# Attention and two MLP blocks on one core: batch 0 takes its first channel group alone, batch 1 follows later, batch 3's heads are spread out

## The chip, the core and the metric

The kernel runs on one core of one Trainium2 chip. Five engines matter. TensorE (PE in the profile, its weight loads PEld) multiplies, VectorE (DVE), ScalarE (ACT) and GpSimd (POOL) work element by element, and SyncE's queue (SP) issues nearly all DMAs. Each engine takes its instructions in one fixed order. The metric is the time of one execution in device microseconds; lower is better.

## The reference, cut to what matters

```
attn = softmax_with_cap(q, k, cap) @ v      # 4 batches, 12 heads, 448 tokens, 64 per head
x    = heads side by side                   # (4, 448, 768)
xn   = (x - mean) / sqrt(var + 1e-6) * g    # over the 768 channels
x    = x + relu(xn @ w_ch1) @ w_ch2         # 768 -> 3072 -> 768
xt   = x transposed                         # tokens last
u    = x + transposed(relu(xt @ w_tok1) @ w_tok2)   # 448 -> 256 -> 448
out  = u + relu(u @ w2_ch1) @ w2_ch2        # 768 -> 1536 -> 768
```

All inputs and outputs are fp32. One batch is one attention, one normalisation, one channel MLP, one token mixing and one second channel MLP, in this order.

## The kernel before

A batch's x lies transposed in SBUF, channels on the partitions in six blocks of 128, tokens along the row (448). Products are made with fp32r operands in three passes: each operand is split into a high part and a low remainder, and high by high, low by high and high by low are added up. Batches 0 and 1 make their attention in plain fp32 (`early`), batches 2 and 3 in split passes.

**Channel MLP.** `mlp(plan, ends)` goes through groups of four hidden blocks. There are six groups in the first MLP (`NG1`) and three in the second (`NG2`). A group is four tiles of `w1` (18 passes of 448 columns for each batch, L541) and six tiles of `w2` (12 passes for each batch, L562), so 144 passes for each batch. What comes out of a `w1` tile is rectified by ACT (L546), and its remainder made by DVE (L547); what comes out of a `w2` tile is added to x by DVE (L566). A plan entry names a group and the batches that take it: a pair such as (0, 1) uses each loaded weight tile twice, a single batch once.

**Weights.** `load` brings a weight tile the first time through `piece`. It loads the raw words (L263), lets ACT work twice (L264, L265) and DVE three times (L266 to L268), then makes the high copy (L164 on ACT or L166 on DVE) and the low remainder on DVE (L160). A `w1` tile is two such pieces of 384 columns, a `w2` tile one of 512, so a group has 14 pieces. The result is kept in DRAM (L288), and every later use of the tile only loads it again (L284). Three split buffers hold tiles at one time.

**Attention.** A head is scores (L351 in fp32, L354 in split passes), tanh and exp on ACT (L357, L358), maxima on DVE (L362, L365), values (L372, or L393 to L396), and two DVE reads of the result (L400, L403). After six heads `divide` spreads the reciprocal sums with three fp32 products (L429) and scales x (L432).

**Normalisation.** `layer_norm` adds the six blocks (L457), subtracts the mean (L447), squares, adds (L469), and takes the root; `normalise` scales (L504) and splits into `big` (L506 and L160). `LN_ENGINES` puts the adds, subtractions and remainders of batch 0 on POOL and those of the others on DVE or POOL as the planner finds.

**Order.** Nothing runs in the order of the code. Each step has a key (`prog.key`, less an `early` lead), and `Program.emit` is a list scheduler with its own costs (`FIXED`, `RATE`). It takes the step whose engine is free first, and among the ready ones that with the least key. The order that comes out is fixed in the program. The keys are set at the end of the kernel, where each stage has a start and a pace.

Before, attention 0 and 1 with their normalisations come first. The pair (0, 1) then goes through all six groups of the first MLP beside the heads of batches 2 and 3, both batches mix tokens together, and the pair takes the second MLP's three groups. After that come the normalisations of batches 2 and 3 and the same for that pair, with batch 2 one group ahead.

Of the kernel before, what the change touches and what calls it, by code (L numbers as in the profile page):

```python
# [9 lines left out]
F32 = mybir.dt.float32  # L10
# [49 lines left out]
URGENT, SCORES, PREPARE, LOAD = 1000.0, 19.31, 4.58, 24.58  # L60
LEAD, RAW_AHEAD, EVACUATE, TOKENS_AHEAD = 6.3, 9.57, -7.49, 17.25
# [10 lines left out]
class Step:  # L72
    def __init__(self, engines, run, key):
        self.engines, self.run, self.key = engines, run, key
        self.waits, self.users, self.ready = 0, [], 0.0
        self.flexible = run.__code__.co_argcount > len(run.__defaults__ or ())


class Program:
# [4 lines left out]
    FIXED = {"pe": 0.0, "act": 0.19, "dve": 0.08, "pool": 0.16, "dma": 0.3}  # L84
    RATE = {"pe": 203e-3 / S, "act": 0.83e-3, "dve": 1.2e-3, "pool": 2.5e-3, "dma": 2.9e-3}
# [5 lines left out]
    def add(self, engine, cols, run, reads=(), writes=(), early=0.0, release=0.0):  # L91
# [3 lines left out]
        names = [name.split("*") for name in engine.split("/")]  # L95
        costs = {e: self.FIXED[e] + self.RATE[e] * cols * (0.5 if half else 1.0) for e, *half in names}
        step = Step(costs, run, (self.key - early, len(self.steps)))
        step.ready = release
# [14 lines left out]
    def emit(self):  # L113
        free = {e: 0.0 for e in self.FIXED}
# [9 lines left out]
        for _ in self.steps:  # L124
# [5 lines left out]
            free[e] = end = t + step.engines[e]  # L130
# [9 lines left out]
def block_kernel(ctx: ExitStack, tc: tile.TileContext, qkv, cap, gln, w1, w2, wt1, wt2, con, out):  # L140
# [116 lines left out]
    def piece(src, m, target, to):  # L257
# [8 lines left out]
        add("dve", m // 2, lambda: dve.tensor_scalar(f, f, 3, None, op0=ALU.logical_shift_left), (), [w])  # L266
        add("dve", m, lambda: dve.scalar_tensor_tensor(f, hi, -(1 << 31), f, op0=ALU.bitwise_and, op1=ALU.bitwise_or), [r], [w])  # L267
        add("dve", m, lambda: dve.tensor_tensor(f, f, lo, op=ALU.add), [r], [w])  # L268
        g = f.bitcast(F32)
        add("act/dve*", m, lambda e: copy(e, target[:, 0], g), [w], to)  # L270
        add("dve", m, lambda e: low(engine_of[e], target[:, 1], g, target[:, 0]), [w], to)
# [45 lines left out]
    def attention(b, start, pace):  # L317
# [7 lines left out]
        def head(h):  # L325
# [3 lines left out]
            add("dma", 960, lambda: nc.sync.dma_start(out=qk.at, in_=qkv[b, h, :, :S + 4 * P]), (), [qk], early=LOAD)  # L329
            add("dma", 384, lambda: nc.sync.dma_start(out=v.at, in_=qkv[b, h, :, S + 4 * P:].rearrange("p (c d) -> p c d", c=4)), (), [v], early=LOAD)  # L330
            q, k = qk.at[:, :S], qk.at[:, S:]
            if not early:
# [3 lines left out]
                add("dve/pool", 4 * P, lambda e: low(engine_of[e], ks.at[D:], k[D:], ks.at[D:]), [qk], [ks], early=PREPARE)  # L336
# [405 lines left out]
```

## Time and profile before

| what | value |
|---|---|
| median of 3 runs | 1439.97 us (1437.99 to 1440.24) |
| the profiled execution | 1440.12 us, of which its span 1438.1 us |
| busy in the span | PE 1397.5, PEld 1186.4, DVE 891.0, ACT 591.7, POOL 153.7 us |
| granted TensorE clock, mean | 0.986 |
| moved by DMA | 230.71 MB, mean 160 GB/s |

The span runs from the first to the last instruction; what lies around it is 2.0 us. Matmuls are pipelined and their records overlap, so the busy time of PE says little by itself: the number of passes in a stretch says more.

### The profile page before, as it was taken

Reading aid. Unit: us, or ns where it says so; the run is one execution under the profiler, and the core shown is the slowest. Engines: PE = TensorE matmul, PEld = TensorE weight load, DVE = VectorE, ACT = ScalarE, POOL = GpSimd, SP = SyncE. Lnnn points to the kernel's source line nnn. Section 1 sums busy time; section 2 is a strip of 40 time slices with the busy share of each in tenths; the row PEclk is TensorE's granted clock in tenths of the full one; section 3 lists DMA queues with packets and bytes.
Section 4 is the critical chain, followed back from the end, with each engine's and each line's share of the span. In section 5 each row is a group of like instructions: output and inputs, shape, how many; then the busy total and the mean of one; then the engine's idle time right before and its main releaser. Section 6 shows DMA issues by size and latency. Waiting matters only on the chain.

```text
span 1438.1 us, 17738 instructions
## 1 busy us (share of the span) xinstructions
PE 1397.5 (97%) x6560; PEld 1186.4 (83%) x6560; DVE 891.0 (62%) x1521; ACT 591.7 (41%) x947; POOL 153.7 (11%) x117
## 2 busy tenths in 40 slices
PE   8998799999999999999999989999999999999998
PEld 3343488888898888878889978999999999999997
DVE  5898799899999898898886883122121222432221
ACT  7885376757664666576543521100101001211000
POOL 0042121112114011011000141000000000000000
PEclk9998899999999999999999999999999999999999
DMA  5564146666574757651475736332332425354366
GB/s 180 166 204 131 38 138 205 214 214 210 184 230 152 249 167 229 193 160 37 141 242 171 238 142 203 103 128 89 116 125 84 130 96 159 126 175 137 118 197 197
DMA packets 116631, 230.71 MB, mean 160 GB/s; under 512 B 9024, under 2 KB 61504, under 8 KB 116544
## 3 DMA queue, kind: packets, MB, share of 16 engines
q1 hardware_dynamic: 115968, 229.28, 49.7%
q8 instruction: 52, 0.85, 0.2%
q10 hardware_dynamic: 576, 0.29, 0.1%
q14 instruction: 35, 0.29, 0.1%
HBM read 167.41 MB, written 62.13 MB: 160 GB/s over the span
## 4 chain that ended last, share of the span: by engine, by line
PE 88%; DVE 8%; DMA 1%; issue 1%; ACT 1%; ACTq 0%; DVEq 0%
PE bank L541 36%; PE bank L562 34%; PE bank L372 4%; PE sc L354 3%; PE bank L636 2%; PE bank L617 2%; PE bank L396 2%; PE bank L395 2%; DVE m L362 1%; PE sc L351 1%; PE bank L429 1%; PE bank L393 1%; DVE whole L267 1%; DVE split L160 1%; DVE area L504 1%
## 5 line engine op out<-in xcount | busy, mean ns | idle before, releaser
L562 PE MATMUL bank<-h,split 128*128 128x448 f32 x2592 | 550.6, 370 | 3.6 <-ACT split L164 1.6
L541 PE MATMUL bank<-big,split 128*128 128x448 f32 x2592 | 548.0, 370 | 4.6 <-DMA split<-kept 1.8
L541 PEld LDWEIGHTS bank<-big,split 128*128 128x128 f32 x2592 | 489.7, 189 | 50.9 <-POOL big L160 2.6
L562 PEld LDWEIGHTS bank<-h,split 128*128 128x128 f32 x2592 | 488.1, 189 | 51.4 <-issue 8.7
L546 ACT ACTIVATE h<-bank 128x448 fp32r<-128x448 f32 x144 | 78.4, 545 | 437.7 <-PE bank L541 437.4
L566 DVE TENSOR_TENSOR x<-x,bank 128x448 f32<-128x448 f32 x216 | 133.4, 618 | 189.8 <-PE bank L562 187.3
L547 DVE SCALAR_TENSOR_TENSOR h<-bank,h 128x448 fp32r<-128x448 f32 x144 | 89.4, 621 | 214.1 <-ACT h L546 213.8
L264 ACT ACTIVATE whole<-raw 128x384 f32<-128x384 f32 (+2 forms) x130 | 77.9, 600 | 54.3 <-DVE split L160 51.0
L164 ACT ACTIVATE split<-whole 128x384 fp32r<-128x384 f32 (+1 forms) x92 | 52.2, 567 | 92.7 <-PE bank L562 63.3
L160 DVE TENSOR_TENSOR split<-whole,split 128x384 fp32r<-128x384 f32 (+1 forms) x126 | 86.5, 690 | 3.9 <-ACT split L164 3.1
L268 DVE CUSTOM_DVE_ANT_0 whole<-raw,whole 128x768 uint16<-128x768 uint16 (+2 forms) x130 | 85.4, 658 | 3.1
L267 DVE SCALAR_TENSOR_TENSOR whole<-raw,whole 128x384 int32<-128x384 int32 (+2 forms) x130 | 85.0, 656 | 0.9
L265 ACT ACTIVATE raw<-raw 128x384 int32<-128x384 uint32 (+2 forms) x130 | 77.5, 598 | 0.0
L160 POOL TENSOR_TENSOR ks<-area,ks 64x512 fp32r<-64x512 f32 x23 | 32.8, 1427 | 351.9 <-ACT ks L335 351.9
L362 DVE TRANSPOSE_TENSOR_REDUCE m<-x 128x28 f32<-128x896 f32 x48 | 52.9, 1104 | 13.9 <-ACT x L358 13.6
L266 DVE TENSOR_SCALAR whole<-whole 128x384 int32<-128x384 int32 (+2 forms) x130 | 57.7, 445 | 4.7 <-ACT whole L264 4.2
L357 ACT ACTIVATE area<-sc,tsc 128x896 f32<-128x896 f32 x48 | 48.4, 1008 | 26.6 <-DVE el L160 13.6
L357 ACT ACTIVATE x<-sc,tsc 128x896 f32<-128x896 f32 x48 | 48.0, 1000 | 21.5 <-PE sc L351 11.0
L362 DVE TRANSPOSE_TENSOR_REDUCE m<-area 128x28 f32<-128x896 f32 x48 | 53.0, 1104 | 5.7 <-ACT area L358 5.7
L358 ACT ACTIVATE x<-x,cap_t 128x896 f32<-128x896 f32 x48 | 49.7, 1040 | 1.0
L358 ACT ACTIVATE area<-area,cap_t 128x896 f32<-128x896 f32 x48 | 49.9, 1040 | 0.4
L380 ACT ACTIVATE eh<-area 128x896 fp32r<-128x896 f32 x48 | 45.4, 946 | 5.8 <-PE bank L395 5.6
(109 smaller groups left out, 1177.3 us busy)
## 6 DMA issues: line engine op xcount, KB each, us to landing
split<-kept SPq DMA_DIRECT2D x96, 384.0 KB, 3.9
split<-kept SPq DMA_DIRECT2D x72, 512.0 KB, 3.7
raw<-in_w SPq DMA_DIRECT2D x72, 384.0 KB, 3.4
kept<-split SPq DMA_DIRECT2D x72, 384.0 KB, 3.2
raw<-in_w SPq DMA_DIRECT2D x54, 512.0 KB, 4.1
kept<-split SPq DMA_DIRECT2D x54, 512.0 KB, 3.3
area<-in_qkv SPq DMA_DIRECT2D x38, 480.0 KB, 3.7
area<-in_qkv SPq DMA_DIRECT2D x35, 192.0 KB, 3.4
```

The costliest lines, as they stand in the source:

```text
L160: eng.tensor_tensor(out, whole, high.bitcast(F32), op=ALU.subtract)
L264: add("act", m, lambda: act(f.bitcast(F32), hi.bitcast(F32), AF.Copy, scale=2.0 ** -112), [r], [w])
L267: add("dve", m, lambda: dve.scalar_tensor_tensor(f, hi, -(1 << 31), f, op0=ALU.bitwise_and, op1=ALU.bitwise_or), [r], [w])
L268: add("dve", m, lambda: dve.tensor_tensor(f, f, lo, op=ALU.add), [r], [w])
L357: add("act", 2 * S, lambda e=e, sc=sc: act(e, sc.at[:, :, :S], AF.Tanh, scale=tsc), [sc], eb)
L358: add("act", 2 * S, lambda e=e: act(e, e, AF.Exp, scale=cap_t), (), eb)
L362: add("dve", 2 * S, lambda half=half, e=e: dve.tensor_reduce(m.at[:, half].rearrange("p c j -> p (c j)"), e.rearrange("p c (j i) -> p (c j ...
L541: mm(ph.at[:, :S], w[:, wi, cc * P:(cc + 1) * P], src[cc].at[:, xi], start=(cc, n) == (0, 0), stop=(cc, n) == (NCC - 1, 2))
L546: add("act", S, lambda ht=ht, ph=ph: act(ht.at[:, 0], ph.at[:, :S], AF.Relu), [ph], [ht], early=EVACUATE)
L547: add("dve", S, lambda ht=ht, ph=ph: dve.scalar_tensor_tensor(ht.at[:, 1], ph.at[:, :S], 0.0, ht.at[:, 0].bitcast(F32), op0=ALU.max, op1=A ...
L562: mm(py.at[:, :S], w[:, wi, i * P:(i + 1) * P], h[i].at[:, hi], start=(i, n) == (0, 0), stop=(i, n) == (G - 1, 2))
L566: add("dve", S, lambda x=x, py=py: dve.tensor_tensor(x.at, x.at, py.at[:, :S], op=ALU.add), [py], [x], early=EVACUATE)
```

## The change

- `prepare(g)` converts the ten tiles of group 0 in advance, from key 14 on, beside attention 0, and keeps them in DRAM.
- Group 0 of the first MLP is taken by batch 0 alone (`groups((0,), 0, n0)`), from key 85, beside attention 1. The pair takes groups 1 to 5.
- Batch 1 takes group 0 while batch 0 mixes tokens. Batch 0 takes the first two groups of the second MLP while batch 1 mixes tokens; the pair takes the third; batch 1 then takes the first two alone.
- Batch 2 now takes two groups ahead (`N1` = 2 in place of 1), the first of them written ahead of batch 3's normalisation.
- The heads of batch 2 get the pace 25 in place of 20.29, those of batch 3 the start 560 and the pace 30 in place of 629.68 and 20.29.
- All of `LN_ENGINES` is DVE.
- In `divide`, the reciprocal sums are split into a high part (ACT) and a low one (DVE), and each of the three products is two fp32r passes in place of one fp32 product.
- The planner's costs change, and steps marked "+" take turns on a port that it now plans for.

```diff
+N0, N1, N2 = 1, 2, 2
+T_LN0, T_LN1 = 7.69, -20.0
+T_AHEAD, N_AHEAD, AHEAD_PACE = 14.0, 1, 5.0
+T_ALONE, STRETCH0, T_PAIR, STRETCH1 = 85.0, 1.3, 165.0, 1.14
+T_ATT2, PACE2, T_ATT3, PACE3 = 171.18, 25.0, 560.0, 30.0
...
+            d = el.at[:NH6]
+            add("act", S, lambda: act(d[:, 0], whole, AF.Copy), [sq], [el])
+            add("dve+", S, lambda: low(dve, d[:, 1], whole, d[:, 0]), [sq], [el])
...
-                    mm(pc.at[:, :S], pair_r[:NH6, pr].bitcast(F32), whole, start=True, stop=True)
+                    for i in range(2):
+                        mm(pc.at[:, :S], pair_r[:NH6, pr], d[:, i], start=i == 0, stop=i == 1)
...
-    LN_ENGINES = ["pool", "dve/pool", "dve/pool", "dve/pool"]
+    LN_ENGINES = ["dve+"] * 4
...
+    def prepare(g):
+        nonlocal n_tile
+        rows = [(w1, g * G + i, C) for i in range(G)] + [(w2, g * NCC + e, G * P) for e in range(NCC)]
+        for w, row, cols in rows:
+            load(n_tile, w, row, cols)
+            n_tile += 1
+            prog.key += AHEAD_PACE
...
-        attention(2, 171.18, 20.29)
+        n0, n1, n2 = N0, N1, N2
+        prog.key, stretch = T_ALONE, STRETCH0
+        weave(mlp(groups((0,), 0, n0)))
+        attention(2, T_ATT2, PACE2)
         layer_norm(2)
-        attention(3, 629.68, 20.29)
-        prog.key, stretch = 152.9, 1.14
-        weave(mlp(groups((0, 1), 0, NG1)))
-        weave(tokens(0, HIDDEN[1]), tokens(1, HIDDEN[2]))
-        weave(mlp(groups((0, 1), NG1, NG2), (0, 1)))
-        prog.key += 59.58
+        attention(3, T_ATT3, PACE3)
+        prog.key, stretch = T_PAIR, STRETCH1
+        weave(mlp(groups((0, 1), n0, NG1 - n0)))
+        weave(tokens(0, HIDDEN[2]), mlp(groups((1,), 0, n0)), ahead=TOKENS_AHEAD)
+        weave(tokens(1, HIDDEN[2]), mlp(groups((0,), NG1, n2)), ahead=TOKENS_AHEAD)
+        weave(mlp(groups((0, 1), NG1 + n2, NG2 - n2), (0,)))
+        weave(mlp(groups((1,), NG1, n2), (1,)))
         normalise(2)
+        stretch = 1.0
+        weave(mlp(groups((2,), 0, n1)))
         layer_norm(3)
         normalise(3)
-        prog.key, stretch = 966.61, 1.0
-        n1, n2 = 1, 2
-        weave(mlp(groups((2,), 0, n1) + groups((2, 3), n1, NG1 - n1)))
+        weave(mlp(groups((2, 3), n1, NG1 - n1)))
```

Three places show how the order moves. The first is TensorE in attention 1, around the sum of the squares of batch 0's normalisation; `sc` and `bank` are PSUM, `big` is the normalised x of batch 0, `split` a weight tile. Before, it stands so:

```order
L474 MATMUL bank_113<-inv_c,area 112x2 x4
L372 MATMUL bank_111<-x_82,x_83 96x448 x2
L372 MATMUL bank_111<-x_83 96x448 x2
L351 MATMUL sc_114<-x_83 128x448 x2
L494 MATMUL bank_112<-area,ones 128x448
L351 MATMUL sc_115<-x_83 128x448 x2
L411 MATMUL bank_110<-kc,rs_103 84x32
L412 MATMUL bank_110<-kc,rm_105 84x128
L351 MATMUL sc_114<-area 128x448 x2
L351 MATMUL sc_115<-area 128x448 x2
L541 MATMUL bank_112<-big_84,split_77 128x448 x6
L429 MATMUL bank_111<-area,pair_r 128x448
```

And now, from the same square sums (L487) on:

```order
L507 MATMUL bank_112<-area,ones 128x448
L360 MATMUL sc_115<-x_83 128x448 x2
L381 MATMUL bank_110<-x_82,x_83 96x448 x4
L360 MATMUL sc_114<-area 128x448 x2
L563 MATMUL bank_112<-big_84,split_78 128x448 x12
L563 MATMUL bank_113<-big_84,split_79 128x448 x12
L360 MATMUL sc_115<-area 128x448 x2
L381 MATMUL bank_111<-x_82,x_83 96x448 x2
L381 MATMUL bank_111<-x_83 96x448 x2
L360 MATMUL sc_114<-x_83 128x448 x2
L360 MATMUL sc_115<-x_83 128x448 x2
L563 MATMUL bank_112<-big_84,split_78 128x448 x6
```

Passes of the MLP (L541 before, L563 now) moved ahead of the sixth head's sums, between the scores and the values of attention 1.

The second place is VectorE at the third and fourth head of attention 0; `m`, `rm` and `rs` are maxima and sums of a head, `whole` and `raw` a weight piece under conversion. Before:

```order
L365 TENSOR_REDUCE rm_104<-m_101 128x14
L362 TENSOR_REDUCE m_100<-x_82 128x28 x2
L400 TENSOR_REDUCE rs_102<-bank_111 32x14
L403 COPY x_80<-bank_111 64x448
L365 TENSOR_REDUCE rm_104<-m_100 128x14
L362 TENSOR_REDUCE m_101<-x_82 128x28
```

And now:

```order
L275 TENSOR_SCALAR whole_75<-whole_75 128x384
L371 TENSOR_REDUCE m_100<-x_82 128x28
L276 SCALAR_TENSOR_TENSOR whole_75<-raw_72,whole_75 128x384
L409 TENSOR_REDUCE rs_102<-bank_111 32x14
L412 COPY x_80<-bank_111 64x448
L277 ISA whole_75<-raw_72,whole_75 128x768
L275 TENSOR_SCALAR whole_76<-whole_76 128x384
L175 CAST split_77<-whole_75 128x384
L276 SCALAR_TENSOR_TENSOR whole_76<-raw_73,whole_76 128x384
L169 TENSOR_TENSOR split_77<-whole_75,split_77 128x384
L277 ISA whole_76<-raw_73,whole_76 128x768
L371 TENSOR_REDUCE m_100<-x_82 128x28
```

Steps of the conversion (L275 to L277, L175, L169) moved in between the maxima of the heads.

The third place is TensorE where batch 1 mixes tokens, now beside batch 0's passes of the second MLP; L636 (now L658) is the mixing's second product, `t` and `h` its weights and hidden rows, L442 are the passes of `divide` for batch 3.

Before, the same second product stands so, the two batches by turns:

```order
L636 MATMUL bank_112<-t_71,h_86 128x448 x3
L636 MATMUL bank_112<-t_71,h_87 128x448 x3
L354 MATMUL sc_115<-qs_95,ks_96 128x448 x4
L636 MATMUL bank_113<-t_71,h_90 128x448 x3
L636 MATMUL bank_113<-t_71,h_91 128x448 x3
L636 MATMUL bank_111<-t_71,h_86 128x448 x3
L636 MATMUL bank_111<-t_71,h_87 128x448 x3
L636 MATMUL bank_112<-t_71,h_90 128x448 x3
```

And now, for batch 1 alone:

```order
L563 MATMUL bank_112<-big_84,split_77 128x448 x12
L563 MATMUL bank_111<-big_84,split_78 128x448 x6
L658 MATMUL bank_112<-t_71,h_92 128x448 x3
L658 MATMUL bank_112<-t_71,h_93 128x448 x3
L563 MATMUL bank_111<-big_84,split_78 128x448 x12
L442 MATMUL bank_110<-el_99,pair_r 128x448 x2
L563 MATMUL bank_113<-big_84,split_79 128x448 x6
L658 MATMUL bank_111<-t_71,h_92 128x448 x3
L658 MATMUL bank_111<-t_71,h_93 128x448 x3
```

No MLP pass stood among the mixing of batches 0 and 1 before. Now passes of batch 0's second MLP moved in between, and batch 0's own mixing is ahead of this place, among batch 1's passes of group 0.

## Rows read from the trace of the kernel before

**Rows 1.** The page's first part: busy us, share of the span, instructions.

```profile
PE 1397.5 (97%) x6560; PEld 1186.4 (83%) x6560; DVE 891.0 (62%) x1521; ACT 591.7 (41%) x947; POOL 153.7 (11%) x117
```

**Rows 2.** Stages: us, busy PE, PEld, DVE, ACT, POOL; clock, DMA share, GB/s.

```profile
8.00:66.00 58.00, 56.96 (x185) 23.05 (x183) 44.17 (x68) 47.34 (x52) 2.60 (x2) 1.00 0.53 174
66.00:126.00 60.00, 53.60 (x174) 23.47 (x173) 57.09 (x96) 46.00 (x63) 25.86 (x21) 0.91 0.53 164
126.00:186.00 60.00, 47.92 (x160) 27.00 (x159) 47.58 (x78) 27.87 (x38) 11.59 (x8) 0.87 0.23 71
...
303.20:381.30 78.10, 78.10 (x374) 68.02 (x373) 72.55 (x121) 53.01 (x85) 16.53 (x10) 1.00 0.60 193
...
618.60:723.70 105.10, 101.74 (x515) 88.59 (x515) 91.99 (x160) 67.86 (x113) 11.95 (x8) 1.00 0.33 105
...
798.80:868.90 70.10, 65.59 (x314) 59.00 (x314) 58.80 (x94) 27.01 (x51) 25.05 (x19) 0.98 0.52 177
868.90:899.30 30.40, 28.57 (x134) 25.99 (x133) 7.27 (x11) 2.26 (x5) 0.72 (x1) 0.94 0.68 222
```

**Rows 3.** The chain that ended last: start us, us, what.

```profile
11.45 2.97 PE bank L372 x7
...
14.79 1.50 PE sc L351 x7
...
51.34 0.95 PE bank L429 x2
...
769.00 29.18 PE bank L562 x144
```

**Rows 4.** The page's fifth part: DVE's four steps of a weight piece.

```profile
L160 DVE TENSOR_TENSOR split<-whole,split 128x384 fp32r<-128x384 f32 (+1 forms) x126 | 86.5, 690 | 3.9 <-ACT split L164 3.1
L268 DVE CUSTOM_DVE_ANT_0 whole<-raw,whole 128x768 uint16<-128x768 uint16 (+2 forms) x130 | 85.4, 658 | 3.1
L267 DVE SCALAR_TENSOR_TENSOR whole<-raw,whole 128x384 int32<-128x384 int32 (+2 forms) x130 | 85.0, 656 | 0.9
...
L266 DVE TENSOR_SCALAR whole<-whole 128x384 int32<-128x384 int32 (+2 forms) x130 | 57.7, 445 | 4.7 <-ACT whole L264 4.2
```

**Rows 5.** Groups by form: busy us, mean ns of one, idle before.

```profile
L362 DVE TRANSPOSE_TENSOR_REDUCE m<-x 128x28 f32<-128x896 f32 x48 | 52.9, 1104 | 13.9 <-ACT x L358 13.6
...
L160 POOL TENSOR_TENSOR qs<-area,qs 128x448 fp32r<-128x448 f32 x23 | 34.4, 1494 | 31.5 <-DVE qs L166 18.5 <-issue 8.1 <-ACT qs L164 3.4
L160 POOL TENSOR_TENSOR ks<-area,ks 64x512 fp32r<-64x512 f32 x23 | 32.8, 1427 | 351.9 <-ACT ks L335 351.9
...
L400 DVE TRANSPOSE_TENSOR_REDUCE rs<-bank 32x14 f32<-32x448 f32 x48 | 31.1, 648 | 21.0 <-PE bank L396 16.0 <-PE bank L372 2.9 <-PE sc L351 1.0
L403 DVE COPY x<-bank 64x448 f32<-64x448 f32 x48 | 29.6, 617 | 0.9
...
L457 DVE TENSOR_TENSOR area<-area,x 128x448 f32<-128x448 f32 x5 | 3.1, 621 | 0.1
```

**Rows 6.** Timeline: start us, us, then the operation.

```profile
88.51 5.18 POOL L447 TENSOR_TENSOR area<-x,mean 128x448 f32<-128x448 f32 x4 [3.81 <-ACT mean L459]
...
88.82 1.25 DVE L160 TENSOR_TENSOR split<-whole,split 128x384 fp32r<-128x384 f32 x1
...
123.83 0.55 DVE L160 TENSOR_TENSOR split<-whole,split 128x384 fp32r<-128x384 f32 x1
...
226.97 0.62 DVE L566 TENSOR_TENSOR x<-x,bank 128x448 f32<-128x448 f32 x1
...
617.99 0.62 DVE L566 TENSOR_TENSOR x<-x,bank 128x448 f32<-128x448 f32 x1 [0.64 <-PE bank L562]
...
868.29 0.61 DVE L566 TENSOR_TENSOR x<-x,bank 128x448 f32<-128x448 f32 x1
```

**Rows 7.** Line 566: least, median and longest ns, first and last start us.

```profile
L566 DVE TENSOR_TENSOR x<-x,bank x216: 581/620/622, 212.3 to 1434.4; 128x448 f32<-128x448 f32 x108
```

**Rows 8.** The busiest 10 us of DMA up to 500 us (columns of rows 2).

```profile
380.00:390.00 10.00, 10.00 (x51) 9.06 (x50) 9.01 (x19) 7.02 (x11) 0.00 (x0) 1.00 0.93 291
```

More of the change, by code (lines that the diff above doesn't have):

```diff
@@ L89, in __init__, with add @@
         self.steps, self.key = [], 0.0
-    def add(self, engine, cols, run, reads=(), writes=(), early=0.0, release=0.0):
-        names = [name.split("*") for name in engine.split("/")]
-        costs = {e: self.FIXED[e] + self.RATE[e] * cols * (0.5 if half else 1.0) for e, *half in names}
+    def add(self, engine, cols, run, reads=(), writes=(), early=0.0):
+        names = [(name.strip("*+"), "*" in name, "+" in name) for name in engine.split("/")]
+        costs = {e: self.FIXED[e] + self.RATE[e] * cols * (0.5 if half else 1.0) for e, half, _ in names}
         step = Step(costs, run, (self.key - early, len(self.steps)))
-        step.ready = release
+        step.port = {e for e, _, port in names if port}
         before = set()
@@ L113, in emit @@
     def emit(self):
-        free = {e: 0.0 for e in self.FIXED}
+        free, port = {e: 0.0 for e in self.FIXED}, 0.0
         queue = {e: [] for e in self.FIXED}
@@ L129, in emit @@
             step.run(e) if step.flexible else step.run()
-            free[e] = end = t + step.engines[e]
+            if e in step.port:
+                t = port = max(t, port) + step.engines[e]
+            else:
+                t += step.engines[e]
+            free[e] = end = t
             end += self.LATER.get(e, 0.0)
@@ L407, in divide @@
             hs = slice(6 * grp, 6 * grp + 6)
-            p, (r,), (sq,) = next(side_banks), R, SQ
+            p, (r,), (sq,), (el,) = next(side_banks), R, SQ, EL
             def gathered():
@@ L567, in mlp @@
                     if b in ends and b in final:
-                        add("dma", S, lambda b=b, e=e, x=x: nc.sync.dma_start(out=out[e, :, b], in_=x.at), [x], ())
+                        add("dma", S // 2, lambda b=b, e=e, x=x: nc.sync.dma_start(out=out[e, :, b], in_=x.at), [x], ())
                     yield
-            if mixing and n_group >= 2:
+            if mixing and len(bs) == 2 and n_group >= 1:
                 prog.key -= LEAD
@@ L669, in block_kernel @@
         setup()
+        prog.key = T_AHEAD
+        for g in range(N_AHEAD):
+            prepare(g)
+        prog.key = 0.0
         attention(0, 0.0, 3.97)
-        prog.key += 7.69
+        prog.key += T_LN0
         layer_norm(0)
@@ L675, in block_kernel @@
         attention(1, 60.01, 6.39)
-        prog.key += 20.53
+        prog.key += T_LN1
         layer_norm(1)
```

43 lines of the change are left out of this document (22 added, 21 removed).

## The prediction

> **What bounds the kernel now.** I read the page's shares first. PE is busy for 97% of the span and no other engine for more than 62% [rows 1], but a busy PE only says that records follow each other. So I counted passes. Where nothing else runs, 144 passes take 29.18 us, 0.2027 us each [rows 3]. With this price, and those of the other matmuls below, I summed all of TensorE's work in its order up to the points where VectorE adds a group's last block to x. I call this PE's ledger. DVE's ledger is the same sum over VectorE's order, with the mean of each form. Before, the eighteenth group of batches 0 and 1 ends at 868.9 us [rows 6]. PE's ledger holds 795 us up to there and DVE's 801 us. What follows, to the end at 1438.1, is 569.2 us against 560.4 us of PE: all work of TensorE, with 9 us lost. So the question is what lies ahead of 868.9.
>
> Rows 2 show three regimes there. In attention 0 (8 to 66) the chain is PE: 1.50 us of scores and 2.97 us of values make 4.5 us and a little more for a head [rows 3], while DVE is busy for 44 of 58 us [rows 2]. From 66 to 126 DVE has 57.1 of 60 us and the clock falls to 0.91. From 126 to 186 nobody is full: DVE 47.6 of 60, PE at a clock of 0.87 [rows 2], since batch 1's normalisation has nothing beside it. PE's ledger to 186 us is some 150 us, so over 30 us of TensorE lie idle, and those the change wants. After 186 both engines are nearly full. In the stage from 303.2 to 381.3 DVE's ledger is 79.4 us for 78.1 us of time, of which DVE was busy for 72.55 [rows 2]. From the addition that ends at 227.6 us to that at 618.6 [rows 6] PE's ledger is 382, DVE's 391, the time 391. I take from this that a stage lasts about as long as the larger of the two ledgers: the 7% by which neighbouring DVE records overlap are about what DVE loses in waits.
>
> **The change, priced.** *DVE's steps of conversion.* A piece costs 690 + 658 + 656 + 445 ns, 2.45 us [rows 4]; group 0's 14 pieces are 34 us. Before, 6 pieces lay ahead of 186 us; now 14 do and some of group 1's. The work moves, it isn't added.
>
> *Normalisation.* Of POOL's 153.7 us, 34.4 + 32.8 are the remainders of q and k, which stay [rows 1, 5]; some 86 us in 66 operations of about 1.3 us go. On DVE one costs 0.62 us [rows 5], so 41 us are added. Against it stands what POOL did to DVE: beside a subtraction on POOL a remainder took 1.25 us, alone 0.55 [rows 6], while the additions from PSUM never exceeded 622 ns [rows 7]. Bounds for the relief are nothing and 0.70 for each of the 66, 46 us. Over all DVE rows of the timeline, those beside a POOL row exceed their like by 48 us for 153.7 us of POOL, 0.31 for each us; I take 27 us. The Trainium skill ("SBUF — State Buffer", section "SBUF: two separate sides") says that the port pair that GpSimd shares with a two-input VectorE operation is held exclusively, and the loser waits for the whole instruction. By that alone the relief could be all 86 us. The rows agree on who is held, but not on how often, and 27 stands.
>
> *divide.* A product cost 0.95 us in attention 0 [rows 3] and is now two passes, 0.41. If the 12 late ones cost no less, 24 products give PE 13 us back; if they cost nothing more than the two passes, 6.5. Half of them stand in the early stage. The ACT copy and the DVE remainder of each of 8 divides (5 us of DVE) lie in a chain that ends in x, with the URGENT lead for the product only; I put it at nothing beyond the ledger, since other heads' work stands between; without that cover it is 1.2 us for each divide.
>
> *Reloads.* Weight loads from DRAM rise from 168 to 238, five groups' worth, in the stretches where one batch goes alone. The one such stretch in rows 2, 868.9 to 899.3, moved 222 GB/s and took 30.4 us for 29.2 of passes. So a single group costs 0 to 1.2 us more; I take 0.7. SP's queue issues them, 14 for each group, ahead of nothing more urgent than the next tile.
>
> Now the stages of the changed order.
>
> **A, up to the last addition of batch 0's lone group.** DVE's ledger: 24 heads of 2 x 1.104 + 0.648 + 0.617 + 0.24 [rows 5], 89 us; 16 pieces, 39; four divides 16; normalisation 0, 20, and the sums of normalisation 1, 10; ten evacuations 6; the rest 4: 184.6 us. PE's is 149. So VectorE now bounds all of it, from the first pieces at about 16 us on. From there 178 us remain. At face value this ends at 194; without POOL beside it the rows are about 5% shorter, and it ends at 185. I take **188**, range 183 to 198. TensorE starves for some 30 us, as before, but 144 passes of batch 0 are then behind it. SP must bring 14 heads (9.6 MB, at 128 x 960 and 128 x 384 words each) and the 14 pieces with their copies back (12.6 MB) in about 93 us, 239 GB/s; the best 10 us of before had 291 [rows 8].
>
> **B, five groups of the pair beside batch 2's heads.** PE 403.5, DVE 413.8. The sums of normalisation 2 leave POOL (17 operations, some 22 us of it), so about 7 us of DVE come off: **407**, bounds 404 and 414.
>
> **C, mixing of batch 0 with batch 1's group 0, mixing of batch 1 with two groups of batch 0, and the pair's last group.** PE 143.8, DVE 169.5, for 38 pieces (93 us) are converted in it while each tile serves one batch alone. Before, the mixings took 105.1 us [rows 2] where PE had 96.6 and DVE 102.3. The stage ahead has slack, PE 50.5 against DVE 42, of which a little carries over: **168**, bounds 147 and 178.
>
> **D, the rest of that group and batch 1's two groups, with normalisation 2 and 3 begun.** PE 89.9, DVE 76. Before, 798.8 to 868.9 lasted 70.1 us [rows 2] for 61 of PE, because batch 3's normalisation had POOL and nothing but the pair's last tiles beside it. Now two more groups stand between. With reloads **93**, bounds 90 and 99.
>
> The eighteenth group ends at 188 + 407 + 168 + 93 = 856 us, in place of 868.9. What follows has the same 560.4 us of PE and two more single groups: 569.2 + 1.4 = 570.6. The span is 1426.6; with 2.0 us around it, as 1440.12 against 1438.1, **1429 us**. The profiled execution lies 0.15 us over the median, so nothing is corrected.
>
> **The rivals.**
>
> *VectorE can't feed single groups (slower).* In C each tile costs DVE 4.9 us (two pieces) and TensorE 3.7 us of passes. If the slack ahead doesn't carry, three split buffers let DVE run no further ahead, and the mixing's own waits come on top as before (8.4 us over PE), C takes 178, and B, which hands over late, its face value of 414. With A and D that is 873, and the end at 1446. For it speaks that DVE's ledger grows by 43 us in all; against it, that from 227.6 to 618.6 the larger ledger was met without loss. It decides against the change once A to C exceed 775 us (763 in my sum).
>
> *The early load doesn't fit (no change).* If the heads of attention 0 wait for loads, at the 174 GB/s of 8 to 66 [rows 2] the 22 MB take 128 us instead of 93. Part of that lies behind DVE's own work; 10 to 15 us later is 1439 to 1444. For it: SP's queue is in order, and copies back that wait for DVE stand ahead of head loads. Against: head loads lead by 24 us of key, and 291 GB/s were seen. The lone group then buys nothing, which is also how it looks if the change only refills what VectorE lacks.
>
> *VectorE is never the bound (much faster).* If the overlap of records holds everywhere, DVE's ledger counts 0.93. Then A ends at 182, B is 404, C 158, D 91: 835, and the end at 1408. Against it: the before showed the ledger met at 1.00.
>
> **How the numbers follow.** Chances: my sum and what lies near it (1413 to 1436) 0.57; much faster 0.13; no change 0.11; slower 0.19. Within 0.2%, 2.9 us, is about what a measurement here can't tell from nothing. So faster 0.70, same 0.11, slower 0.19. My sum's own bounds are 183 + 404 + 147 + 90 and 198 + 414 + 178 + 99, but they don't fall together; 1415 to 1443 is what two of them at once allow. To leave out no more than 2 in 10 the range goes to 1410 and 1447.
>
> **What would show it.** Batch 0's last lone addition (L588's sixth) near 188 us, DVE busy for over 94% from 20 to 188, POOL silent there. The eighteenth group's last addition near 856. In C, DVE over 92% and PE with gaps ended by DVE's split remainders. Behind it some 571 us of nearly gapless passes. I am wrong if A ends after 200 (then SP's or DVE's order is to blame), if C takes over 178, or if TensorE shows no gap in C at all.

## The result, and the profile after

The changed kernel takes 1416.28 us (median of four, 1414.58 to 1421.1), the kernel before 1438.98: a ratio of 0.9848, interval 0.9822 to 0.9875. It is faster by 22.7 us where 11 were forecast. The profiled execution is the slowest of the four, 1421.1 us with a span of 1419.3; the last section says what most of its extra 5 us are. Executions in a slower state, 280 us and more above the others, are left out of every number in this document.

The page's first part of the changed kernel, against [rows 1]:

```profile
PE 1389.8 (98%) x6560; PEld 1179.0 (83%) x6560; DVE 889.8 (63%) x1589; ACT 599.4 (42%) x961; POOL 66.2 (5%) x51
```

POOL lost 87.5 us, and VectorE, with 68 instructions more, is no longer busy than before. Next the stage marks, from VectorE's timeline: the additions (now L588) that end batch 0's lone group, the twelfth group and the eighteenth (a group counts once for each batch that takes it), against the L566 rows of [rows 6]:

```profile
188.03 0.61 DVE L588 TENSOR_TENSOR x<-x,bank 128x448 f32<-128x448 f32 x1
...
601.96 0.61 DVE L588 TENSOR_TENSOR x<-x,bank 128x448 f32<-128x448 f32 x1
...
844.71 0.62 DVE L588 TENSOR_TENSOR x<-x,bank 128x448 f32<-128x448 f32 x1
```

The eighteenth group ends at 845.3 us, not 868.9: 23.6 us earlier, so the whole gain lies ahead of it, as the prediction held. The windows by stage, in the columns of [rows 2] (A is the first three rows, then B, C and D; B ends with the twelfth group, C with the sixth addition of the pair's last group):

```profile
8.00:66.00 58.00, 54.94 (x182) 21.79 (x181) 53.30 (x97) 55.09 (x74) 0.00 (x0) 1.00 0.86 294
66.00:126.00 60.00, 50.89 (x158) 22.40 (x157) 57.35 (x107) 42.75 (x56) 0.00 (x0) 0.89 0.63 200
126.00:188.60 62.60, 61.65 (x247) 39.63 (x246) 53.07 (x91) 34.48 (x47) 2.54 (x2) 1.00 0.51 156
188.60:602.60 414.00, 411.28 (x2003) 363.82 (x2003) 369.74 (x666) 269.92 (x444) 49.30 (x33) 1.00 0.63 202
602.60:754.40 151.80, 148.01 (x735) 131.92 (x734) 144.06 (x274) 99.67 (x179) 11.28 (x8) 1.00 0.75 245
754.40:845.30 90.90, 90.67 (x441) 79.30 (x440) 71.49 (x128) 35.48 (x52) 2.51 (x2) 1.00 0.56 180
```

A ended at 188.6 (188 forecast), B lasted 413.9 (407), C 151.8 (168), D 90.9 (93). These are the stretches that the forecast's numbers were summed over, but its words draw B and C otherwise: the twelfth group is batch 1's group 0, which ran beside batch 0's transposes and first products from 551.2 to 602.6 us, in B. C begins with the second products of batch 0's mixing. The forecast names all of this under C.

Between 126 and 188.6, where the kernel before had TensorE at a clock of 0.87 and busy for 48 of 60 us, TensorE is now full at 1.00. C is the surprise. In it VectorE is busy for 144.1 of 151.8 us, and its largest groups in this window (L276, L277, L169 on `split` and L275 are the four steps of [rows 4]) are:

```profile
L276 DVE SCALAR_TENSOR_TENSOR whole<-raw,whole 128x384 int32<-128x384 int32 (+1 forms) x38 | 25.5, 672 | 0.0
L277 DVE CUSTOM_DVE_ANT_0 whole<-raw,whole 128x768 uint16<-128x768 uint16 (+1 forms) x38 | 24.8, 652 | 0.2
L169 DVE TENSOR_TENSOR split<-whole,split 128x384 fp32r<-128x384 f32 (+1 forms) x38 | 24.1, 634 | 0.3 <-ACT split L173 0.3
L275 DVE TENSOR_SCALAR whole<-whole 128x384 int32<-128x384 int32 (+1 forms) x38 | 14.6, 384 | 0.7 <-ACT whole L273 0.6
...
L371 DVE TRANSPOSE_TENSOR_REDUCE m<-area 128x28 f32<-128x896 f32 x7 | 7.7, 1103 | 0.1
...
L169 DVE TENSOR_TENSOR el<-area,eh 128x896 fp32r<-128x896 f32 (+1 forms) x6 | 5.1, 852 | 0.0
```

The 38 pieces counted in advance are there, at 2.34 us each (priced 2.45). The durations of all 274 instructions in C add up to 163.5 us. That is more than the 151.8 us that C lasted: neighbouring records overlap, and VectorE got through 1.08 us of rows for each us of time. All that TensorE waits for in C is VectorE, but little, 3.7 us:

```profile
PE bank L658 <- DVE h L569: 1.0, 1, 1.0
PE bank L584 <- DVE split L169: 0.9, 1, 0.9
PE bank L584 <- DVE x L588: 0.9, 1, 0.9
PE bank L563 <- DVE split L169: 0.7, 2, 0.4
PE bank L658 <- DVE h L645: 0.2, 1, 0.2
```

So VectorE doesn't hold C by itself. The chain that ended last runs in C mostly over TensorE; its shares by line:

```profile
by line: PE bank L563 29.2%; PE bank L584 24.9%; PE bank L658 6.4%; PE bank L639 3.9%; DVE whole L276 3.5%; DVE whole L277 3.2%; DVE split L169 2.8%; PE sc L363 2.7%; DVE big L169 2.5%; DMA kept<-split 2.2%; issue 2.0%; PE bank L405 1.9%; P
```

Added up by engine, TensorE has 110.9 of the 151.8 us and VectorE 33.4; in B TensorE has 404.8 of 413.9.

### The profile page after: what moved, and what is told of

The parts are those of the page before. It is cut to its first block, busy times and chain, and to the rows that moved or that the text cites. A ratio compares the mean times of both kernels' runs of the same rounds, so it can differ in the third digit from the quotient of the medians.

```text
span 1419.3 us, 17844 instructions
## 1 busy us (share of the span) xinstructions
PE 1389.8 (98%) x6560; PEld 1179.0 (83%) x6560; DVE 889.8 (63%) x1589; ACT 599.4 (42%) x961; POOL 66.2 (5%) x51
## 4 chain that ended last, share of the span: by engine, by line
PE 89%; DVE 7%; DMA 2%; ACT 1%; issue 1%; SPq 0%; ACTq 0%; DVEq 0%
PE bank L584 36%; PE bank L563 36%; PE sc L363 3%; PE bank L381 3%; PE bank L639 2%; PE bank L658 2%; PE bank L405 2%; PE bank L404 2%; PE sc L360 1%; PE bank L402 1%; DVE m L371 1%; DVE split L169 1%; DMA split<-kept 1%; DVE whole L276 1%; PE bank L615 1%
## 5 line engine op out<-in xcount | busy, mean ns | idle before, releaser
L563 PE MATMUL bank<-big,split 128*128 128x448 f32 x2592 | 551.4, 369 | 4.8 <-DVE split L169 2.6
L563 PEld LDWEIGHTS bank<-big,split 128*128 128x128 f32 x2592 | 485.4, 188 | 54.7 <-DVE split L169 4.2
L588 DVE TENSOR_TENSOR x<-x,bank 128x448 f32<-128x448 f32 x216 | 133.2, 618 | 187.5 <-PE bank L584 185.8
L277 DVE CUSTOM_DVE_ANT_0 whole<-raw,whole 128x768 uint16<-128x768 uint16 (+2 forms) x130 | 83.3, 641 | 0.5
L276 DVE SCALAR_TENSOR_TENSOR whole<-raw,whole 128x384 int32<-128x384 int32 (+2 forms) x130 | 81.8, 630 | 0.2
L169 DVE TENSOR_TENSOR split<-whole,split 128x384 fp32r<-128x384 f32 (+1 forms) x126 | 80.0, 636 | 2.0 <-ACT split L173 1.6
L169 POOL TENSOR_TENSOR ks<-area,ks 64x512 fp32r<-64x512 f32 x24 | 36.7, 1529 | 690.2 <-ACT ks L344 670.6
L275 DVE TENSOR_SCALAR whole<-whole 128x384 int32<-128x384 int32 (+2 forms) x130 | 55.2, 427 | 1.9 <-ACT whole L273 1.7
```

Source lines behind the costliest of these rows:

```text
L169: eng.tensor_tensor(out, whole, high.bitcast(F32), op=ALU.subtract)
L276: add("dve+", m, lambda: dve.scalar_tensor_tensor(f, hi, -(1 << 31), f, op0=ALU.bitwise_and, op1=ALU.bitwise_or), [r], [w])
L277: add("dve+", m, lambda: dve.tensor_tensor(f, f, lo, op=ALU.add), [r], [w])
L563: mm(ph.at[:, :S], w[:, wi, cc * P:(cc + 1) * P], src[cc].at[:, xi], start=(cc, n) == (0, 0), stop=(cc, n) == (NCC - 1, 2))
L588: add("dve", S, lambda x=x, py=py: dve.tensor_tensor(x.at, x.at, py.at[:, :S], op=ALU.add), [py], [x], early=EVACUATE)
```

## The experiments

Times are medians, with the ratio to the kernel before on the same chip; a stage is read from the profiled execution. What follows the eighteenth group took 567.6 to 574.0 us in the profiles, whatever the edit (the last section shows a part of the reason), so an effect is read better from the marks than from a median. The changed kernel again, on two other chips, gave 1421.35 (0.9862, interval 0.9833 to 0.989) and 1415.97 us (0.9844, 0.9831 to 0.9857), and its stages came out within 0.5 us each time. Stage A came out near 188.5 or 190.5 us in kernels that don't differ there; 2 us in A are not counted as an effect.

### One part of the change taken back, or made alone

**All normalisations back on POOL.**

```diff
-    LN_ENGINES = ["dve+"] * 4
+    LN_ENGINES = ["pool", "dve/pool", "dve/pool", "dve/pool"]
```

The "+" goes too, as in the kernel before: the planner no longer counts these operations on its port.

> The changed kernel with the normalisation's 64 operations on POOL once more, for its trace by stage; 10 to 18 us over the changed kernel. Theory A: POOL's hold on VectorE costs, so the stages lengthen where POOL works, the first (to 188.6 us) by 5 to 8 and the pair's groups by 2 to 4. Theory B: it is the chain of a normalisation, twice as long on POOL, that others wait for, so nearly all of the loss stands at the last one (772.9 to 845.3 us), 8 us or more.

1438.1 us, 0.9984 (0.9964 to 1.0003); on another chip 1432.94, 0.9951 (0.9925 to 0.9977), without a profile by stage. Nearly the whole gain is gone, some 16 us in the median and 17 at the eighteenth group. B, C and D of this kernel:

```profile
191.70:609.80 418.10, 411.93 (x1995) 362.46 (x1995) 370.44 (x639) 267.94 (x436) 74.72 (x52) 1.00 0.62 200
609.80:771.30 161.50, 153.72 (x753) 136.01 (x752) 152.79 (x281) 107.41 (x192) 16.83 (x12) 0.99 0.72 234
771.30:862.40 91.10, 88.75 (x423) 77.76 (x422) 60.88 (x99) 28.04 (x42) 19.43 (x14) 0.98 0.56 177
```

Against the changed kernel A is 3 us longer, B 4, C 9.7, D the same. Theory B put nearly all of it at the last normalisation, in D, and fell; theory A named the first two, but not C.

**The same on the kernel before: its normalisations on VectorE, nothing else.**

```diff
-    LN_ENGINES = ["pool", "dve/pool", "dve/pool", "dve/pool"]
+    LN_ENGINES = ["dve"] * 4
```

> The kernel before, with the one change that all of the normalisation is on DVE. Theory: VectorE loses no time by this and the normalisation's own chain gets shorter (0.62 us for 1.3 us an operation), above all between 820 and 870 us: faster by 6 to 14 us, 1425 to 1433. Rival: VectorE is the bound, and 41 us more of work on it make it slower or equal: 1437 to 1446.

1426.4 us, 0.9889 (0.9864 to 0.9915): one line gives about two thirds of the gain. Here it comes at the other end. The stretch that took 70.1 us before (798.8 to 868.9 in [rows 2]) now takes 59.1, with TensorE full:

```profile
795.80:854.90 59.10, 59.10 (x296) 54.54 (x295) 47.92 (x88) 24.00 (x45) 0.00 (x0) 1.00 0.59 203
```

There the normalisations of batches 2 and 3 were a chain of POOL operations of twice VectorE's length with little beside them. In the changed order other groups stand beside that chain: with the normalisations of batches 2 and 3 given back to POOL (below), TensorE is busy for 94.63 of D's 94.9 us. So the same edit pays for different things in the two orders.

**No lone group, no early conversion** (batches 0 and 1 go as a pair from group 0).

```diff
-N0, N1, N2 = 1, 2, 2
+N0, N1, N2 = 0, 2, 2
...
-T_AHEAD, N_AHEAD, AHEAD_PACE = 14.0, 1, 5.0
+T_AHEAD, N_AHEAD, AHEAD_PACE = 14.0, 0, 5.0
```

> The changed kernel, but without the lone group: batch 0 does not take group 0 alone, nothing is converted in advance, the pair takes all six groups, and batch 0's mixing has no group beside it. Theory: the lone group fills TensorE's idle time in attention 1, worth 10 to 16 us: 1426 to 1432. Rival: the gain lies in the later stages (single groups among the mixings, batch 3's spread heads, the transition), so this keeps most of it: 1414 to 1420.

1425.85 us, 0.9886 (0.9858 to 0.9914). The eighteenth group ends at 857.1.

**The old pace of the heads of batches 2 and 3.**

```diff
-T_ATT2, PACE2, T_ATT3, PACE3 = 171.18, 25.0, 560.0, 30.0
+T_ATT2, PACE2, T_ATT3, PACE3 = 171.18, 20.29, 629.68, 20.29
```

> The changed kernel with the old starts and paces of batch 2's and 3's heads (20.29 us each, batch 3 from 629.68). Theory: VectorE bounds the stretch of the mixings, and heads that come denser there cost it 5 to 12 us: 1421 to 1428. Rival: the order is set by what is ready, not by the pace: within 3 us of the changed kernel.

1424.72 us, 0.9879 (0.9854 to 0.9903). B takes 428.6, C 156.3, D 81.2; the eighteenth group ends at 854.5. Each of the three parts, taken back, thus moves that mark by 9 to 17 us, 38 in all, where the whole change moved it by 23.6: the parts don't add.

**The normalisations of one half of the batches back.** Batches 0 and 1:

```diff
-    LN_ENGINES = ["dve+"] * 4
+    LN_ENGINES = ["pool", "dve+/pool+", "dve+", "dve+"]
```

> The changed kernel with the normalisations of batches 0 and 1 given back to POOL; those of batches 2 and 3 stay on VectorE. If the halves add up, this one carries the rest of the 17 us: 1428 to 1432, with stage A 3 us later and the rest of it in B and C. If the loss of both together comes from the order (in it, VectorE has the same heads ahead of stage C's start and end as the changed kernel), only A's 3 us and the hold beside it are lost: 1418 to 1423, with C at 152.

1421.11 us, 0.9875 (0.9855 to 0.9896). Batches 2 and 3, in two runs:

```diff
-    LN_ENGINES = ["dve+"] * 4
+    LN_ENGINES = ["dve+", "dve+", "dve+/pool+", "dve+/pool+"]
```

> The changed kernel with the normalisations of batches 2 and 3 given to POOL or VectorE as before; those of batches 0 and 1 stay on VectorE. All four given back cost 15 to 17 us. If the loss sits where VectorE is full (attention 0 and 1 and stage B), this costs 8 us or less. If it sits in the long chain of batch 3's normalisation and in what batch 2's sums push into stage C: 12 us or more.

> The other half again: 1417 to 1421. In the profile stage A near 188, B with POOL busier by some 20 us and 1 to 4 us longer, C with half a head less than in the changed kernel, 148 to 152, and D, which then holds a head more and batch 3's sums on POOL, 92 to 96.

1417.95 us, 0.9854 (0.9838 to 0.987), without a profile by stage, and 1418.87, 0.985 (0.9831 to 0.9868), with B, C and D as follows:

```profile
190.60:600.40 409.80, 406.25 (x1985) 359.70 (x1983) 363.36 (x640) 262.82 (x433) 71.50 (x49) 1.00 0.61 201
600.40:752.80 152.40, 147.65 (x731) 131.54 (x732) 143.14 (x274) 100.61 (x181) 14.61 (x11) 1.00 0.75 247
752.80:847.70 94.90, 94.63 (x460) 82.28 (x459) 68.46 (x107) 38.46 (x54) 26.05 (x19) 1.00 0.58 185
```

With a half given back, the eighteenth group ends 2 to 4 us later, with both 17. But the two edits differ in one thing more: the halves keep the "+" (batch 0 has none in either), so their order takes POOL's turns on the port into account, and the order with both halves back doesn't. No run gave both back with the "+".

POOL's hold on VectorE does not make this difference. The sum of all of VectorE's row durations is 971.9 us in the changed kernel. It is 966.8 with one half on POOL (40 operations fewer on VectorE, 25 us), 959.1 with the other (34, 21 us) and 959.9 with both (62, 39 us), so the rows that are left grew by 20, 8 and 27 us: the hold adds up. And the kernel with batches 2 and 3 on POOL has POOL as busy in B as the one with both halves (71.5 against 74.7 us) and goes through B 8 us faster. So the hold can't be the whole of the 17 us; the rest comes with the order. Counting in VectorE's order shows part of it. In B it does 17 heads here and 18 there, in C three and four, in D four and two. A head is about 6 us of VectorE: in the rows of C above two maxima make 2.2 us and two remainders of `el` 1.7, the rest is smaller. D is the one of these stages in which VectorE has time to spare (71.5 of 90.9 us), and which heads fall into it comes out of the list scheduler.

### Work added to VectorE and to POOL

**VectorE's last conversion step made twice for the second MLP's 42 pieces** (some 25 us).

```diff
...
-        add("dve+", m, lambda e: low(engine_of[e], target[:, 1], g, target[:, 0]), [w], to)
+        for _ in range(times):
+            add("dve+", m, lambda e: low(engine_of[e], target[:, 1], g, target[:, 0]), [w], to)
...
```

> The changed kernel with VectorE's last step of a conversion (the low remainder) done twice for the second MLP's 42 pieces, which are converted while the batches mix tokens: some 25 us more of VectorE there. Theory: VectorE bounds that stretch (it is busy for 95% of the 152 us from 602.6 to 754.4), only at a lower price than the prediction's sum of means, so the time grows by 15 to 25 us: 1431 to 1441. Rival: TensorE's passes bound it, with VectorE's load hidden: within 6 us of the changed kernel.

1430.69 us, 0.993 (0.9905 to 0.9956). Its window of C:

```profile
602.50:766.80 164.30, 151.46 (x723) 133.06 (x722) 155.16 (x299) 99.62 (x182) 6.47 (x5) 0.97 0.68 223
```

and TensorE's longest waits there:

```profile
PE bank L585 <- DVE split L169: 6.1, 4, 2.1
PE bank L564 <- DVE split L169: 3.6, 5, 1.4
```

C grows by 12.5 us, and TensorE now waits for the doubled step, 9.7 us against 1.6. VectorE's rows in C grew by 13 us and not by 24, because one and a half heads left it, and some 5 of the 12.5 us are TensorE's clock, which was 1.00 and is a mean of 0.97. The eighteenth group ends 16 us later, within what was expected; the median is only 9 us above the changed kernel's on the same chip.

**Thirty subtractions more, on POOL or on VectorE**, one behind each addition in the mixings' single groups and the pair's last group; nobody reads the result (the second kernel has "dve" where the first has "pool").

```diff
...
+                    if extra:
+                        add("pool", S, lambda x=x: engine_of["pool"].tensor_tensor(scr.at, x.at, x.at, op=ALU.subtract), [x], [scr])
...
```

> The changed kernel with 30 subtractions of 128 x 448 added on POOL, one behind each addition to x in the mixings' single groups and the pair's last group (60 to 75 per cent of them inside stage C); what they write is read by nobody. 30 x 1.3 us is 39 us of POOL and no VectorE work. If an operation on POOL holds VectorE up for about its whole length, some 31 us are taken from VectorE in stage C, and at the rate at which the doubled remainders cost time there (25 us of VectorE for some 16 us) C grows by about 20 us: 1435 to 1442. At the prediction's 0.31 us for each us of POOL it is 12 us of VectorE and 8 us of time: about 1426. If POOL does not hold VectorE up at all: 1417 to 1420.

> The same 30 subtractions at the same places, on VectorE: 30 x 0.62 us, 18.6 us of VectorE and none of POOL. If stage C is VectorE's to bound, at the rate of the doubled remainders: 12 us more, about 1430, most of it in C. If C has slack on VectorE, no more than 3 us: 1418 to 1421. Beside the run with the operations on POOL this says which engine is the dearer place for one: with a full hold POOL's costs about twice as much, with 0.31 two thirds as much.

On POOL 1422.66 us, 0.9856 (0.9826 to 0.9885); on VectorE 1422.41, 0.9858 (0.9831 to 0.9885). C of the first and of the second:

```profile
604.30:761.50 157.20, 149.71 (x741) 133.09 (x740) 151.28 (x271) 102.05 (x184) 34.95 (x26) 1.00 0.72 236
```

```profile
601.40:758.80 157.40, 150.23 (x726) 131.01 (x725) 150.15 (x291) 98.98 (x180) 8.37 (x6) 0.99 0.72 236
```

Both move the eighteenth group's mark by some 8 us (852.8 and 853.2), of which 2 lie in A. The theory that POOL holds VectorE for the whole of its operation expected 20 us in C for the first; C grew by 5. The sum of VectorE's rows rose by 8.7 us (980.6 for 971.9) for 38.6 us of POOL, 0.23. Thirty such operations cost the kernel the same on either engine, although VectorE takes 0.62 us for one and POOL 1.26.

**The remainders of q and k on VectorE too**, so that POOL does nothing after the start.

```diff
...
-                add("dve+/pool+", 4 * P, lambda e: low(engine_of[e], ks.at[D:], k[D:], ks.at[D:]), [qk], [ks], early=PREPARE)
+                add("dve+", 4 * P, lambda e: low(engine_of[e], ks.at[D:], k[D:], ks.at[D:]), [qk], [ks], early=PREPARE)
...
```

The remainders of q (`qs`) are changed in the same way.

> The changed kernel with the remainders of q and k on VectorE too, so that POOL does nothing after the start. 52 operations go, some 64 us of POOL; VectorE gets about 30 us. If POOL's operations hold VectorE up for about their whole length, VectorE wins some 30 us net, and stage B falls from 414 towards TensorE's 404 and C by some us: about 1406. At 0.31 VectorE gets 10 us more to do: 1422 to 1428. If POOL costs VectorE nothing, 30 us more: about 1440.

1415.67 us, 0.9807 (0.978 to 0.9833). Its first part:

```profile
PE 1384.8 (98%) x6560; PEld 1180.9 (84%) x6560; DVE 891.4 (63%) x1639; ACT 595.8 (42%) x956; POOL 0.6 (0%) x6
```

Fifty operations more for VectorE, 31 us at 0.62, and the sum of its rows rises by 3.1 (975.0 for 971.9): 65.6 us of POOL had lengthened its rows by 28, 0.43. The stages end within 4 us of the changed kernel's, so neither the full hold (1406) nor no hold (1440) fits.

### Where the pieces are converted

**Three `w1` tiles of the second MLP converted earlier,** beside batch 0's mixing.

```diff
...
-        weave(tokens(0, HIDDEN[2]), mlp(groups((1,), 0, n0)), ahead=TOKENS_AHEAD)
+        weave(tokens(0, HIDDEN[2]), beside(mlp(groups((1,), 0, n0)), [(w1, NG1 * G + i, C) for i in range(3)]), ahead=TOKENS_AHEAD)
```

> The changed kernel, with three w1 tiles of the second MLP's first group (6 pieces, some 12 us of VectorE) converted earlier, among batch 1's group 0 beside batch 0's mixing, and only loaded again later. The stretch ahead has VectorE busy for 40 of 51 us. Theory (VectorE bounds the mixings): 3 to 8 us faster than the changed kernel, 1408 to 1414. Rival: the tiles only take up split buffers and loads: equal or up to 6 us slower.

1426.46 us, 0.9903 (0.9877 to 0.9929). That is some 5 us slower than the changed kernel on the same chip, as the rival had it. The order shows what came with it: batch 3 has five heads in C in place of 3.5, and two in D. C takes 161.3 us, with a clock of 0.98:

```profile
605.30:766.60 161.30, 156.84 (x761) 138.75 (x760) 148.37 (x271) 106.65 (x185) 13.80 (x10) 0.98 0.66 217
```

**The lone group without the early conversion.**

```diff
-T_AHEAD, N_AHEAD, AHEAD_PACE = 14.0, 1, 5.0
+T_AHEAD, N_AHEAD, AHEAD_PACE = 14.0, 0, 5.0
```

> The changed kernel without the early conversion: the lone group stays, its 14 pieces are converted when it runs, in attention 1. If the early conversion is what lets the lone group fit (VectorE had 44 of 58 us in attention 0 and 57 of 60 in attention 1), stage A ends some 10 us later and most of it stays: about 1424, near the kernel without a lone group (1426). If the pieces find room behind the normalisation: 1417 to 1421.

> The changed kernel without the early conversion, again, beside the changed kernel. If the early conversion crowds VectorE in attention 1 (its 14 pieces make maxima late, scores wait for them and the clock falls), stage A ends near 178 again and the kernel is 5 us faster than the changed one. If the first reading was the chip's, both are the same within 2 us.

1414.85 us, 0.9795 (0.9767 to 0.9823); and beside the changed kernel on one chip 1414.22 (1409.40 to 1414.76) against its 1415.97 (1415.65 to 1417.68). A's last addition, ten us earlier, of which B hands back half:

```profile
177.72 0.61 DVE L588 TENSOR_TENSOR x<-x,bank 128x448 f32<-128x448 f32 x1
```

This is the opposite of what I had expected. The windows of attention 1, first in the changed kernel:

```profile
66.00:90.00 24.00, 20.25 (x64) 7.90 (x62) 23.66 (x44) 17.92 (x23) 0.00 (x0) 1.00 0.80 253
90.00:126.00 36.00, 30.64 (x94) 14.50 (x95) 33.69 (x64) 24.83 (x33) 0.00 (x0) 0.81 0.51 165
```

What TensorE and ACT wait for in it, from 66 to 126 us:

```profile
PE sc L360 <- ACT x L366: 6.3, 4, 3.6
...
ACT x L366 <- DVE m L371: 7.3, 7, 2.0
```

The same windows without the early conversion:

```profile
66.00:90.00 24.00, 23.56 (x79) 9.58 (x79) 22.58 (x41) 17.38 (x20) 0.00 (x0) 1.00 0.51 159
90.00:126.00 36.00, 33.92 (x138) 19.43 (x137) 34.94 (x70) 28.88 (x43) 0.00 (x0) 1.00 0.44 137
```

With the early pieces VectorE is full (23.66 of 24 us). ACT waits for its maxima before it may overwrite x, TensorE for ACT before the next scores. TensorE idles for 3.75 us, and behind that the granted clock, 1.00 until then, falls to 0.81 over the next 36 us, a mean of stretches at 2.4 and at 1.2 GHz, which costs TensorE 6.8 us. Without them TensorE is busy for 23.56 of 24 us and keeps the clock. That the idle time is what drops the clock is read from this order of events, not tried by itself.

**Both:** no early conversion and nothing on POOL.

> Without the early conversion and with the remainders of q and k on VectorE, so that POOL does nothing. If POOL's hold on VectorE is worth what VectorE gets to do (as the run with all on VectorE said: 30 us added, busy time 1.6 us up), it is the same as without the early conversion, within 2 us. If the two add up by another 4 us or more, the hold is dearer where VectorE has less to do in attention 1.

1414.9 us, 0.9828 (0.9809 to 0.9848): the same as without the early conversion alone, which is the best kernel measured here: 1 to 2 us below the changed one in the median, 6 at the end of the eighteenth group.

## Why the prediction came out as it did

The kernels with the changed plan fit one reading of C. The table is worked out: VectorE's summed rows in C, C's time, their quotient, and the heads of batches 2 and 3 that VectorE's order has in B, C and D (counted by their maxima, two to a head), with the end of the eighteenth group. The kernel with all normalisations on POOL is the one without the "+".

```
kernel                      rows     C  quot.   heads B/C/D    end
changed                    163.5 151.8  1.08   17.5/3.5/3    845.3
all on VectorE             162.6 151.2  1.08   17/3/4        843.4
no early conversion        164.6 152.0  1.08   17.5/3.5/3    839.5
LN of 2, 3 on POOL         162.5 152.4  1.07   17/3/4        847.7
LN of 0, 1 on POOL         161.9 156.5  1.03   17.5/3.5/3    848.9
30 operations on POOL      170.5 157.2  1.08   17.5/3.5/3    852.8
30 operations on VectorE   172.0 157.4  1.09   17/3/4        853.2
old pace                   168.1 156.3  1.08   19/5/0        854.5
three tiles earlier        167.1 161.3  1.04   17/5/2        852.8
all LN on POOL             172.5 161.5  1.07   18/4/2        862.4
doubled remainder          176.5 164.3  1.07   17.5/2/4.5    861.4
```

C lasts as long as VectorE's rows, divided by 1.03 to 1.09. A head that moves brings TensorE passes as well as VectorE rows, so most lines of the table don't tell the two engines apart. The three with work added do: C grew by 5 to 13 us with no passes more in the program. No kernel here has clearly fewer rows in C, so it isn't shown that C would get shorter with them. The two lowest quotients, 1.03 and 1.04, are those of kernels whose granted clock was 0.98 in C (three tiles earlier, above, and the normalisations of 0 and 1 on POOL), some 3 us of TensorE in each. The clock isn't all of it, for the doubled remainder had 0.97 and a quotient of 1.07. C with the normalisations of 0 and 1 on POOL:

```profile
601.90:758.40 156.50, 151.91 (x739) 135.14 (x738) 144.11 (x272) 102.82 (x186) 10.94 (x8) 0.98 0.74 239
```

**The step that failed** is the rule "a stage lasts about as long as the larger of the two ledgers", with its reason that the overlap of VectorE's records "is about what DVE loses in waits", as far as it made VectorE's ledger the floor of C. I had it from stretches of before, such as the one where 391 us of rows took 391 us. But there TensorE was nearly full too, with 382 us. In C, VectorE got through 163.5 us of rows in 151.8, 1.08 us of rows in 1 us: the records overlapped as before, but VectorE waited for 7.7 us only, and the waits that were to eat the overlap up did not come. For C that means: ledger 169.5; the rows' own durations after 163.5 (6 us by shorter rows); divided by 1.08, 151.8. I forecast 168. The 16 us are most of the miss of 12.7; B's 7 us go the other way. What sets C's length instead is open. TensorE's ledger of 143.8 with the 8 us on top that the mixings lost before (105.1 for 96.6) comes to the same 152, and C's chain is mostly TensorE's; the runs with work added say that VectorE has next to no slack under it. The third rival ("VectorE is never the bound") had this overlap, and its C of 158 was the nearest, but it let it hold in A and B too. The sign named for C, VectorE busy for over 92% and gaps of TensorE ended by split remainders, came true (95%, gaps of 1.6 us) although C was 16 us shorter: it could not tell these two readings apart.

**A** was right in number, 188.6, in part by luck, for its reason was wrong. VectorE was full to 126 us, but busy for 155.9 of the 168.6 us from 20 to 188.6, 92% and not 94: in the last third TensorE was. Nearly the same VectorE rows without the early conversion (177.8 against 180.1 us) end A at 178.3. So the ledger did not set A's end. The second rival was right that the early conversion costs 10 us, and wrong that the load does: loads ran at 294 GB/s from 8 to 66 us, no wait of TensorE's passes in A is put down to a DMA, and the longest ends with ACT, which waits for VectorE.

**B**, 413.9, with TensorE busy for 411.28 us, came out at the ledger's face value; the 7 us that I took off for POOL's sums did not come. With those sums back on POOL, B was not longer (409.8, with half a head less in it). VectorE's ledger of before, 801 us up to 868.9, was too low: its rows up to there add up to 818.

**D** was right: 90.9 for 93, TensorE full, batch 3's normalisation covered by the groups beside it.

**The relief by POOL**, booked at 27 us or 0.31 for each us, was about right, and somewhat low. On the kernel before, where the normalisations alone changed sides, 66 operations (41 us) came to VectorE and the sum of its rows rose by 5.9 us (965.5 for 959.6): 35 us for 85 us of POOL, 0.41. In the changed kernel the same move gave 27 us, 0.32. The runs with work added to POOL and with none on it gave 0.23 and 0.43. The Trainium skill ("SBUF — State Buffer", section "SBUF: two separate sides") has the loser of the shared port wait for the whole instruction; no run here came near 1. By that rule a POOL operation would have met an operation that needs the port in less than half of its time; the rows don't show which these are.

**The first rival** fell: A to C together ended at 754.4, where 775 would have decided against the change. **The tail**, forecast at 570.6, was 574.0 in the profiled execution and 568.0 and 570.1 in the other two.

**Where the gain comes from** has no sum by parts. The kernel before loses TensorE time in three places: attention 1's end, VectorE's full stages, and the last normalisations. Each part of the change helps at more than one of them. Shown is that the normalisations' move alone gives about two thirds, and that each of the three parts, taken back, costs 9 to 17 us at the eighteenth group. The planner's costs and its port, `divide`'s split products and the groups woven among the mixings were not taken back by themselves. Why the halves of the normalisations' move cost 2 to 4 us and the whole 17 stays open: the heads' places go with the 8 and 9 us of B and C against the half's run, but the "+" differs too, and no run fixed either while moving the normalisations.

## What to carry to other kernels

A sum of row durations is not a time, and no floor of one: compare it with the time where that engine is busy nearly throughout (95% in C), not where another engine is full beside it. Moving work into an engine's free time by a scheduler moves other work as well; count in the order which steps changed stages before putting a gain or a loss down to the edit. Converting early isn't free when the engine that converts is also the one that frees the buffers of the running stage.

## What the runs showed of the hardware

Passes of one shape run at two rates under the same granted clock. In the stretch where batches 2 and 3 go as a pair, the chain of the changed kernel's first profile has

```profile
994.42 29.76 PE bank L584 x144
1024.18 29.76 PE bank L563 x144
```

and the same kernel on another chip has

```profile
991.72 29.18 PE bank L584 x144
1020.90 29.18 PE bank L563 x144
```

with a granted clock of 1.00 in both: 206.7 or 202.7 ns for a pass, 2%. The kernel before has 29.18 us at 769.00 [rows 3]. The changed kernel's other two profiles have 202.7 ns there and 206.7 later on. The seven stretches that differ, 0.58 us each, are 4 of the 5 us by which the profiled execution of the first lies above the median. No run tells what sets the rate.

The other thing is the price of an operation on POOL: thirty of 1.26 us moved the end of the eighteenth group by 7.5 us, thirty of 0.62 us on VectorE by 7.9.
